# Attention followed by a gated MLP: one PSUM buffer of eight banks, two of them read side by side

## The chip, the core and the metric

The kernel runs on one core of one Trainium2 chip. The metric is device time in microseconds (us) of the one launch, as a median of several runs; smaller is better. The core has five engines with a queue each: PE multiplies matrices and writes its results to PSUM; ACT (ScalarE) and DVE (VectorE) read PSUM and write SBUF, the working memory; POOL (GpSimd) works on SBUF; SP issues DMAs. In this kernel PSUM is used as eight banks of 128 partitions by 512 fp32 columns. PE, ACT, DVE and POOL work their queues in program order, and wait for one another through semaphores.

## The reference

Grouped-query attention and then a gated MLP with a mixing over the sequence. Eight batches, 16 query heads in 4 groups, 384 positions, head size 64; the inner widths are 1024 and 512.

```python
scores = scale * np.matmul(q, k.transpose(0, 1, 3, 2))      # k, v repeated for the 4 heads of a group
attn = np.exp(scores - np.max(scores, axis=-1, keepdims=True))
attn = attn / (np.sum(attn, axis=-1, keepdims=True) + 1e-09)
x = np.matmul(attn, v)                    # heads side by side: (8, 384, 1024)
...
h = np.maximum(x @ w_in, 0.0)
u, v = h[..., :512], h[..., 512:]
v_n = (v - mu) / np.sqrt(var + 1e-06)     # mean and variance over the 512
v_s = np.einsum('ts,bsd->btd', w_spatial, v_n) + b_spatial[None, :, None]
return (u * v_s) @ w_out
```

## The kernel before

**Tiles.** A batch's attention is cut into six *sets*: three blocks of 128 query rows, times two pairs of key/value heads. One set has three *units*, one for each block of 128 keys. In a unit PE makes scores for the two halves of the pair (`hh` 0 and 1): two matmuls of 64 rows by 512 columns, one on rows 0 to 63 of the array and one on rows 64 to 127, so that they run side by side, each into a bank of its own (`sc`, L281). ACT takes the exponential of each bank into the tile `aT` (L293; no maximum is subtracted, which a count at the end of the kernel guards). `weigh` then multiplies `aT` with the values: 12 matmuls of 65 columns for each half into one bank `av` (L301); the 65th column of each head is the sum of the weights. DVE takes the reciprocals of these sums (L315) and multiplies (L317) into `x16`, which goes on to the MLP transposed, by PE for the first batch (`x_turn`), by a DMA on SP's queue for the others (`x_send`).

**The MLP is filler.** A generator (`gated`, L514) yields the MLP's matmuls one by one: `pv` (L357, the half that is normalized; DVE takes its relu and statistics), `pu` (L438; ACT takes the relu), `psp` (L457, the mixing over positions; DVE adds the bias, POOL multiplies by u) and `po` (L496, the output; DVE or ACT copies it, and SP sends it out). Each of these holds a bank from its first matmul until its reader is done, and `pour` (L727) stops in mid-accumulation wherever the share of work that it was given is used up.

**The order is written out by hand** (L53: the schedule is manual). The loop over the first 21 units (L749) issues a unit or two, then transposes and other things that are due, then weighs half a set, then pours. The loop after that (L774) goes by sets: the six score matmuls of a set; the three exponentials of half 0; a pour of 0.2 of a step's share; the weighing of the *second* half of the set before; a pour of 0.3; whatever is due; the three exponentials of half 1; a pour of 0.1; the weighing of the *first* half of this set; a pour of 0.4.

**Banks are planned.** `bank` (L79) gives out PSUM by a small clock of its own: it keeps for each bank when its reader will be done (`done`), takes the one that is done first, and moves PE's clock there if it isn't yet. `spend` (L87) moves PE's clock by a matmul's cost, `reads` (L90) the reader's. These costs only decide which bank is taken and how much is poured; on the chip the waits are semaphores. Each bank is a tile of its own with a tag, so a matmul that writes a bank waits for whatever read it last.

Of the kernel before, what the change touches and what calls it, by code (L numbers as in the profile page):

```python
# [18 lines left out]
def kernel(  # L19
# [14 lines left out]
    nc = tc.nc  # L34
    P = 128
    B, HQ, S, D = q.shape
# [18 lines left out]
    cst = ctx.enter_context(tc.tile_pool(name="cst", bufs=1))  # L55
# [5 lines left out]
    ps = order.enter_context(tc.tile_pool(name="ps", bufs=1, space=PSUM))  # L61
# [7 lines left out]
            name=nc.get_next_instruction_name(), act_func_set_id=set_id, ins=[], outs=[]  # L69
        )  # L70
    )
    pool, dve, act, sp = nc.gpsimd, nc.vector, nc.scalar, nc.sync


    clock = {nc.tensor: 7700.0, act: 0.0, dve: 0.0}
    done = [0.0] * 8
    taken = {}

    def bank(shape, dtype, name):  # L79
        i = min(range(8), key=done.__getitem__)  # L80
        t = ps.tile(shape, dtype, name=name, tag=f"bank{i}")
        clock[nc.tensor] = max(clock[nc.tensor], done[i])
        done[i] = 1e12 + clock[nc.tensor]
        taken[name] = i
        return t

    def spend(ns):  # L87
        clock[nc.tensor] += ns

    def reads(eng, ns, name=None):  # L90
        clock[eng] = max(clock[eng], clock[nc.tensor] + 200.0) + ns
        if name:
            done[taken.pop(name)] = clock[eng]

    C512, C384, C128 = 216, 162, 56

# [78 lines left out]
    v1 = [cst.tile([P, HKV, NT, VW], FP16, name=f"v1_{i}") for i in range(2)]  # L175
# [4 lines left out]
    k16s, q16s, kTs, qTs = {}, {}, {}, {}  # L180
# [35 lines left out]
    def copy(eng, o, i, name):  # L216
        reads(eng, 600.0 if name.startswith("po") else 430.0, name)
        (act.copy if eng is act else dve.tensor_copy)(o, i)  # L218
# [45 lines left out]
    aTs, x16s, xts = {}, {}, {}  # L264
    r_all = cst.tile([P, B * SETS * 2 * G], FP32, name="r_all")

    def units(u, count):
        b, r = divmod(u, UNITS)
        s, kt0 = divmod(r, NT)
        qt, j = divmod(s, 2)  # L270
        kts = range(kt0, kt0 + count)
        if kt0 == 0:
            aTs[b, s] = att.tile([P, NT, 2, G * P], FP16, name=f"aT_{b}_{s}", tag="aT", bufs=3)
        scs = [
            (kt, hh, bank([P, G * P], FP32, f"sc_{b}_{s}_{hh}_{kt}"))
            for hh in range(2)
            for kt in kts
        ]
        for kt, hh, sc in sorted(scs, key=lambda x: x[:2]):
            rows = slice(hh * D, (hh + 1) * D)  # L280
            nc.tensor.matmul(  # L281
                sc,
                kTs[b][rows, j, kt * P : (kt + 1) * P],
                qTs[b, j][rows, qt].rearrange("p (r i c) -> p i r c", r=G, i=G),
                start=True,
                stop=True,
            )
        spend(count * C512 + 186)
        return [(aTs[b, s][:, kt, hh], sc, f"sc_{b}_{s}_{hh}_{kt}") for kt, hh, sc in scs]

    def exp(a, sc, name):
        reads(act, 480.0, name)
        act.activation(a, sc, AF.Exp, scale=scale)  # L293

    def weigh(b, s, hh):
        qt, j = divmod(s, 2)
        aT = aTs[b, s]
        av = bank([P, 512], FP32, f"av_{b}_{s}_{hh}")
        for kt in range(NT):
            for i in range(G):  # L300
                nc.tensor.matmul(  # L301
                    av[:, i * (D + 1) : (i + 1) * (D + 1)],
                    aT[:, kt, hh, i * P : (i + 1) * P],
                    v1[b % 2][:, 2 * j + hh, kt, 0 : D + 1],
                    start=(kt == 0 and i == 0),
                    stop=(kt == NT - 1 and i == G - 1),
                )
        if s == 0 and hh == 0:
            x16s[b] = att.tile([P, NT, DM], FP16, name=f"x16_{b}", tag="x16")
        o = av[:, 0 : G * (D + 1)].rearrange("p (i d) -> p i d", i=G)  # L310
        spend(372)
        n = (b * SETS + s) * 2 + hh
        r = r_all[:, n * G : (n + 1) * G].rearrange("p (i a) -> p i a", a=1)
        reads(dve, 600.0, f"av_{b}_{s}_{hh}")
        dve.reciprocal(r, o[:, :, D : D + 1])  # L315
        c = j * 512 + hh * 256
        dve.tensor_tensor(  # L317
            x16s[b][:, qt, c : c + 256].rearrange("p (i d) -> p i d", i=G),
            o[:, :, 0:D],
            r.to_broadcast([P, G, D]),  # L320
            ALU.mult,
        )
        measure()

    def new_xt(b):
# [278 lines left out]
    def idle(count):  # L604
        name = f"idle_{idle_no[0]}"
        ps = bank([P, P], FP32, name)
        done[taken.pop(name)] = clock[nc.tensor] + 400.0
# [113 lines left out]
    ends = {}  # L721
# [25 lines left out]
    halves = {}  # L747
    TWO = 13
    for u in range(ALONE):  # L749
        if u < TWO or (u - TWO) % 2 == 0:  # L750
            pairs = units(u, 1)
            if u >= TWO and u + 1 < ALONE:
                pairs += units(u + 1, 1)
            for pair in pairs:
                exp(*pair)
        spare = 736 if u < TWO else (600 if (u - TWO) % 2 == 0 else 870)
        for f, args in todo.pop(u, []):
            f(*args)
            spare -= 224 if f in (q_turn, x_turn, k_turn) else 0
        for b, s in ends.pop(u, []):  # L760
            halves.setdefault(u, []).append((b, s, 0))
            halves.setdefault(u + (0 if s == 0 else 1), []).append((b, s, 1))
        for h in halves.pop(u, []):
            weigh(*h)
            spare -= 372
            if h[2]:
                turn_x(*h[:2], u)
        owed = pour(u, min(owed, 0) + spare)
    for u in sorted(halves):
        for h in halves[u]:  # L770
            weigh(*h)
    owed = 0.0
    late = [(b, s, hh) for u in (ALONE, ALONE + 1) for b, s in ends.pop(u, []) for hh in range(2)]
    for n in range(ALONE, total, NT):  # L774
        share = STEP * (0.85 if n < 90 else 1.0)
        exps = units(n, NT)
        for pair in exps[:NT]:
            exp(*pair)
        owed = pour(n, owed + share * F[0])
        for h in late:  # L780
            weigh(*h)
            if h[2]:
                turn_x(*h[:2], n)
        owed = pour(n, owed + share * F[1])
        for u in range(n, n + NT):
            for f, args in todo.pop(u, []):
                f(*args)
        for pair in exps[NT:]:
            exp(*pair)
# [7 lines left out]
    for h in late:  # L797
        weigh(*h)
        turn_x(*h[:2], n)
# [240 lines left out]
```

## Time and profile before

| | |
|---|---|
| time, median of 3 runs | 238.28 us (238.16 to 238.79) |
| time of the profiled execution | 238.65 us |
| its span, first to last instruction | 237.1 us |
| granted TensorE clock | 1.00 |
| instructions | 5954 |
| DMA traffic | 47.48 MB, mean 200 GB/s |

The span is 1.5 us shorter than the execution's time. The busy time in tenths, in 40 slices of 5.9 us each, shows how the engines are loaded over time:

| | |
|---|---|
| PE | 7899999999999999999999999999999999999993 |
| DVE | 2668774676447674566646576376744667367561 |
| ACT | 2899989959897869977797776986697776401212 |

In the first slices, up to some 30 us, ACT is as full as PE: many units, little filler. From there to some 200 us a step for each set repeats with a period of 4.0 to 4.6 us. After the last set only the MLP of the last two batches is left, and ACT is nearly idle. A row of a group in the profile gives an instruction's line, engine, what it writes and reads, its count, its total busy time and the mean of one in ns, then the idle time of the engine ahead of it and what ended that.

### The profile page before, as it was taken

Reading aid. Unit: us, or ns where it says so; the run is one execution under the profiler, and the core shown is the slowest. Engines: PE = TensorE matmul, PEld = TensorE weight load, DVE = VectorE, ACT = ScalarE, POOL = GpSimd, SP = SyncE. Lnnn points to the kernel's source line nnn. Section 1 sums busy time; section 2 is a strip of 40 time slices with the busy share of each in tenths; the row PEclk is TensorE's granted clock in tenths of the full one; section 3 lists DMA queues with packets and bytes.
Section 4 is the critical chain, followed back from the end, with each engine's and each line's share of the span. In section 5 each row is a group of like instructions: output and inputs, shape, how many; then the busy total and the mean of one; then the engine's idle time right before and its main releaser. Section 6 shows DMA issues by size and latency. Waiting matters only on the chain.

```text
span 237.1 us, 5954 instructions
## 1 busy us (share of the span) xinstructions
PE 230.4 (97%) x2317; PEld 124.3 (52%) x2317; DVE 143.8 (61%) x382; ACT 170.0 (72%) x350; POOL 102.2 (43%) x149
## 2 busy tenths in 40 slices
PE   7899999999999999999999999999999999999993
PEld 6555655545554545555464555554465455545542
DVE  2668774676447674566646576376744667367561
ACT  2899989959897869977797776986697776401212
POOL 3489493642556442275045800575032500460740
PEclk9999999999999999999999999999999999999999
DMA  6999959999999999699988899479912543240266
GB/s 186 289 300 308 275 152 160 169 317 260 296 211 237 258 351 171 214 199 309 188 257 214 241 214 294 68 271 158 255 27 44 114 164 79 48 177 0 86 229 222
DMA packets 67757, 47.48 MB, mean 200 GB/s; under 512 B 48368, under 2 KB 60576, under 8 KB 67728
## 3 DMA queue, kind: packets, MB, share of 16 engines
q1 hardware_dynamic: 62800, 39.86, 68.9%
q0 software_dynamic: 3952, 6.42, 12.3%
q10 hardware_dynamic: 976, 0.82, 1.1%
q8 instruction: 18, 0.29, 0.5%
q14 instruction: 11, 0.09, 0.1%
HBM read 25.95 MB, written 12.58 MB: 163 GB/s over the span
## 4 chain that ended last, share of the span: by engine, by line
PE 91%; DMA 4%; DVE 2%; issue 0%; ACTq 0%; ACT 0%
PE pu L438 18%; PE pv L357 17%; PE po L496 17%; PE sc L281 15%; PE av L301 14%; PE psp L457 7%; DMA q<-in_q_dram 2%; DMA qT<-q 2%; PE qps L240 1%; PE xps L334 1%; DVE x L317 1%; DVE qT L218 0%; DVE osb L218 0%; DVE q L208 0%; ACTq L124 0%
## 5 line engine op out<-in xcount | busy, mean ns | idle before, releaser
L293 ACT ACTIVATE aT<-sc 128x512 f16<-128x512 f32 x288 | 147.5, 617 | 31.4 <-PE sc L281 30.8
L301 PEld LDWEIGHTS <-aT 128*128 128x128 f16 x1152 | 47.0, 97 | 17.3 <-issue 2.3
L357 PE MATMUL pv<-w_in,xt 128*128 128x512 f16 x192 | 51.0, 380 | 0.1
L301 PE MATMUL av<-v,aT 128*128 128x65 f16 x1152 | 50.5, 193 | 0.1
L496 PE MATMUL po<-w_out,gT 128*128 128x512 f16 (+2 forms) x200 | 50.5, 371 | 0.0
L438 PE MATMUL pu<-xt,w_in 128*128 128x384 f16 x256 | 49.9, 327 | 0.0
L401 POOL TENSOR_SCALAR vn<-vr,rstd,nmr 128x512 f16<-128x512 f32 x23 | 17.6, 779 | 67.0 <-DVE nmr L396 45.6
L474 POOL TENSOR_TENSOR gT<-vs,uT 128x384 f16<-128x384 f32 x31 | 32.4, 1058 | 31.8 <-DVE r_all L315 16.9
L317 DVE TENSOR_TENSOR x<-av,r_all 128x256 f16<-128x256 f32 x96 | 40.7, 424 | 3.3
L281 PE MATMUL sc<-qT,kT 64*128 64x512 f16 x288 | 41.5, 380 | 0.3
L315 DVE RECIPROCAL r_all<-av 128x4 f32<-128x4 f32 x96 | 17.1, 178 | 40.6 <-PE av L301 40.3
L218 DVE COPY osb<-po 128x512 f32<-128x512 f32 (+2 forms) x39 | 26.1, 669 | 16.3 <-PE po L496 16.3
L438 PEld LDWEIGHTS <-w_in 128*128 128x128 f16 x256 | 22.1, 98 | 17.1 <-issue 5.5
L449 ACT ACTIVATE uT<-pu 128x384 f16<-128x384 f32 x32 | 15.8, 495 | 16.0 <-PE pu L438 15.8
L496 PEld LDWEIGHTS <-gT 128*128 128x128 f16 x200 | 17.6, 98 | 17.1 <-issue 3.3
L357 PEld LDWEIGHTS <-xt 128*128 128x128 f16 x192 | 15.8, 97 | 17.8 <-issue 5.5
L281 PEld LDWEIGHTS <-kT 64*128 64x128 f16 x288 | 10.9, 94 | 23.5 <-issue 11.9
L457 PE MATMUL psp<-wsT,vn 128*128 128x384 f16 x96 | 22.2, 327 | 0.0
L469 DVE TENSOR_TENSOR vs<-psp,bias_bc 128x384 f32<-128x384 f32 x32 | 17.6, 552 | 7.1 <-PE psp L457 6.9
L371 DVE TENSOR_SCALAR vr<-pv 128x512 f32<-128x512 f32 x24 | 16.4, 682 | 8.4 <-PE pv L357 8.3
L203 POOL CAST q<-q 128x768 f16<-128x768 f32 x22 | 17.6, 830 | 7.9 <-issue 4.3
L383 DVE BATCH_NORM_STATS2 stats<-vr 128x6 f32<-128x512 f32 x24 | 16.4, 685 | 0.1
(55 smaller groups left out, 103.2 us busy)
## 6 DMA issues: line engine op xcount, KB each, us to landing
out_dram<-osb SPq DMA_DIRECT2D x20, 512.0 KB, 3.9
q<-in_q_dram SPq DMA_DIRECT2D x10, 768.0 KB, 5.7
v_None<-in_v_dram SPq DMA_DIRECT2D x6, 384.0 KB, 7.0
w_in<-in_moe_w_in_dram POOLq DMA_DIRECT2D x4, 512.0 KB, 9.8
k_None<-in_k_dram SPq DMA_DIRECT2D x5, 384.0 KB, 3.8
out_dram<-osb SPq DMA_DIRECT2D x7, 256.0 KB, 2.5
q<-in_q_dram POOLq DMA_DIRECT2D x2, 768.0 KB, 7.6
w_out<-in_moe_w_out_dram POOLq DMA_DIRECT2D x2, 512.0 KB, 9.5
```

The costliest lines, as they stand in the source:

```text
L203: eng.tensor_copy(t16[:, :, :, hh, :], src[:, hh])
L218: (act.copy if eng is act else dve.tensor_copy)(o, i)
L281: nc.tensor.matmul(sc, kTs[b][rows, j, kt * P : (kt + 1) * P], qTs[b, j][rows, qt].rearrange("p (r i c) -> p i r c", r=G, i=G), start=True ...
L293: act.activation(a, sc, AF.Exp, scale=scale)
L301: nc.tensor.matmul(av[:, i * (D + 1) : (i + 1) * (D + 1)], aT[:, kt, hh, i * P : (i + 1) * P], v1[b % 2][:, 2 * j + hh, kt, 0 : D + 1], st ...
L317: dve.tensor_tensor(x16s[b][:, qt, c : c + 256].rearrange("p (i d) -> p i d", i=G), o[:, :, 0:D], r.to_broadcast([P, G, D]), ALU.mult,)
L357: nc.tensor.matmul(pv, xts[b][:, kt, st * P : (st + 1) * P], w_in16[:, kt, DH:DFF], start=(kt == 0), stop=(kt == NK - 1),)
L401: (dve if b == 0 and st == 1 else pool).tensor_scalar(vn, v_r.pop((b, st)), rstd[:, st : st + 1], nmr[:, st : st + 1], op0=ALU.mult, op1=A ...
L438: nc.tensor.matmul(pu[:, 0:S], w_in16[:, kt, m * P : (m + 1) * P], xts[b][:, kt, :], start=(kt == 0), stop=(kt == NK - 1),)
L457: nc.tensor.matmul(psp[:, 0:S], v_n[b, st][:, m * P : (m + 1) * P], wsT16[:, st, :], start=(st == 0), stop=(st == NT - 1),)
L474: pool.tensor_tensor(gT, vs, uT, ALU.mult)
L496: nc.tensor.matmul(po[:, 0:width], gTs[b][:, m, tt * P : (tt + 1) * P], w_out16[:, m, c0 : c0 + width], start=(m == 0), stop=(m == NM - 1),)
```

## The change

PSUM becomes one tensor of eight banks. `bank` gives out one of them, and now prefers, among those that its clock holds to be free, one whose neighbour will be busy longest. `pair` gives out two neighbours, or, if these would be free over 300 ns later than the two best, any two. A unit's two halves go into a pair, and one exponential reads both (1024 columns); where no neighbours were had, two exponentials do. `weigh` takes both halves of a set in a row into a pair, and DVE makes one reciprocal and one product of both. In the loop over sets the first two units' exponentials stand at the front and the third in the middle, and the whole set before is weighed in the one place where its second half was; the shares of filler 0.1 and 0.4 behind the last exponential become one of 0.5. In the first 21 units both halves are weighed at the unit where the first was. The planner's costs are 840 ns for a wide exponential (960 for two) and 900 ns for the wide reciprocal and product (1200 for two).

```diff
+    psum = ps.tile([P, 8, 512], FP32, name="psum")
...
     def bank(shape, dtype, name):
-        i = min(range(8), key=done.__getitem__)
-        t = ps.tile(shape, dtype, name=name, tag=f"bank{i}")
...
+        free = [i for i in range(8) if done[i] <= clock[nc.tensor]]
+        i = max(free, key=lambda i: done[i ^ 1]) if free else min(range(8), key=done.__getitem__)
+        hold(name, i)
+        t = psum[:, i]
...
+    def pair(name):
+
+        i = min(range(7), key=lambda i: max(done[i : i + 2]))
+        j, k = sorted(range(8), key=done.__getitem__)[:2]
+        if max(done[i : i + 2]) > max(done[k], clock[nc.tensor]) + 300.0:
+            hold(name, j, k)
+            return [psum[:, j], psum[:, k]], None
+        hold(name, i, i + 1)
+        return [psum[:, i], psum[:, i + 1]], psum[:, i : i + 2]
...
-    def exp(a, sc, name):
-        reads(act, 480.0, name)
-        act.activation(a, sc, AF.Exp, scale=scale)
-
-    def weigh(b, s, hh):
+    def exp(a, two, both, name):
+        if both is not None:
+            reads(act, 840.0, name)
+            act.activation(a, both, AF.Exp, scale=scale)
+        else:
+            reads(act, 960.0, name)
+            for hh in range(2):
+                act.activation(a[:, hh], two[hh], AF.Exp, scale=scale)
...
+    def weigh(b, s):
...
+        two, both = pair(name)
+        for hh in range(2):
+            for kt in range(NT):
+                for i in range(G):
+                    nc.tensor.matmul(
+                        two[hh][:, i * (D + 1) : (i + 1) * (D + 1)],
+                        aT[:, kt, hh, i * P : (i + 1) * P],
+                        v1[b % 2][:, 2 * j + hh, kt, 0 : D + 1],
...
+            dve.reciprocal(r[:, h0:h1], o[:, :, :, D : D + 1])
+            dve.tensor_tensor(
+                x[:, h0:h1], o[:, :, :, 0:D], r[:, h0:h1].to_broadcast([P, h1 - h0, G, D]), ALU.mult
+            )
...
         exps = units(n, NT)
-        for pair in exps[:NT]:
-            exp(*pair)
+        for x in exps[:2]:
+            exp(*x)
         owed = pour(n, owed + share * F[0])
-        for h in late:
-            weigh(*h)
-            if h[2]:
-                turn_x(*h[:2], n)
+        for x in late:
+            weigh(*x)
+            turn_x(*x, n)
         owed = pour(n, owed + share * F[1])
...
-        for pair in exps[NT:]:
-            exp(*pair)
-        owed = pour(n, owed + share * F[2])
-        late = []
-        for u in range(n, n + NT):
-            for b, s in ends.pop(u + 2, []):
-                weigh(b, s, 0)
-                late.append((b, s, 1))
-        owed = pour(n, owed + share * F[3])
+        for x in exps[2:]:
+            exp(*x)
+        owed = pour(n, owed + share * (F[2] + F[3]))
+        late = [x for u in range(n, n + NT) for x in ends.pop(u + 2, [])]
```

More of the change, by code (lines that the diff above doesn't have):

```diff
@@ L92, in reads @@
         if name:
-            done[taken.pop(name)] = clock[eng]
+            for i in taken.pop(name):
+                done[i] = clock[eng]
     C512, C384, C128 = 216, 162, 56
@@ L273, in units @@
             aTs[b, s] = att.tile([P, NT, 2, G * P], FP16, name=f"aT_{b}_{s}", tag="aT", bufs=3)
[L274 to L287, printed above, removed]
@@ L288, in units @@
-        spend(count * C512 + 186)
-        return [(aTs[b, s][:, kt, hh], sc, f"sc_{b}_{s}_{hh}_{kt}") for kt, hh, sc in scs]
-    def exp(a, sc, name):
-        reads(act, 480.0, name)
-        act.activation(a, sc, AF.Exp, scale=scale)
-    def weigh(b, s, hh):
+        scs = [(kt, *pair(f"sc_{b}_{s}_{kt}")) for kt in kts]
+        for kt, two, _ in scs:
+            for hh, sc in enumerate(two):
+                rows = slice(hh * D, (hh + 1) * D)
+                nc.tensor.matmul(
+                    sc,
+                    kTs[b][rows, j, kt * P : (kt + 1) * P],
+                    qTs[b, j][rows, qt].rearrange("p (r i c) -> p i r c", r=G, i=G),
+                    start=True,
+                    stop=True,
+                )
@@ new lines, in units @@
+        spend(count * C512 + 186)
+        return [(aTs[b, s][:, kt], two, both, f"sc_{b}_{s}_{kt}") for kt, two, both in scs]
+    def exp(a, two, both, name):
+        if both is not None:
+            reads(act, 840.0, name)
+            act.activation(a, both, AF.Exp, scale=scale)
+        else:
+            reads(act, 960.0, name)
+            for hh in range(2):
+                act.activation(a[:, hh], two[hh], AF.Exp, scale=scale)
+    r_all = cst.tile([P, B * SETS * 2 * G], FP32, name="r_all")
@@ L296, in weigh @@
+    def weigh(b, s):
         qt, j = divmod(s, 2)
         aT = aTs[b, s]
[L298 to L307, printed above, removed]
@@ L308, in weigh @@
-        if s == 0 and hh == 0:
-            x16s[b] = att.tile([P, NT, DM], FP16, name=f"x16_{b}", tag="x16")
[L310 to L322, printed above, removed]
+        name = f"av_{b}_{s}"
@@ new lines, in weigh @@
+        if s == 0:
+            x16s[b] = att.tile([P, NT, DM], FP16, name=f"x16_{b}", tag="x16")
+        spend(744)
+        n = (b * SETS + s) * 2 * G
+        r = r_all[:, n : n + 2 * G].rearrange("p (h i a) -> p h i a", h=2, a=1)
+        x = x16s[b][:, qt, j * 512 : j * 512 + 512].rearrange("p (h i d) -> p h i d", h=2, i=G)
+        reads(dve, 900.0 if both is not None else 1200.0, name)
+        for h0, h1, av in ((0, 2, both),) if both is not None else ((0, 1, two[0]), (1, 2, two[1])):
+            if both is None:
+                av = av.rearrange("p (h f) -> p h f", h=1)
+            o = av[:, :, 0 : G * (D + 1)].rearrange("p h (i d) -> p h i d", i=G)
+            dve.reciprocal(r[:, h0:h1], o[:, :, :, D : D + 1])
+            dve.tensor_tensor(
+                x[:, h0:h1], o[:, :, :, 0:D], r[:, h0:h1].to_broadcast([P, h1 - h0, G, D]), ALU.mult
+            )
@@ L606, in idle @@
         ps = bank([P, P], FP32, name)
-        done[taken.pop(name)] = clock[nc.tensor] + 400.0
+        for i in taken.pop(name):
+            done[i] = clock[nc.tensor] + 400.0
         idle_no[0] += 1
@@ L750 @@
         if u < TWO or (u - TWO) % 2 == 0:
-            pairs = units(u, 1)
+            exps = units(u, 1)
             if u >= TWO and u + 1 < ALONE:
-                pairs += units(u + 1, 1)
-            for pair in pairs:
-                exp(*pair)
+                exps += units(u + 1, 1)
+            for x in exps:
+                exp(*x)
         spare = 736 if u < TWO else (600 if (u - TWO) % 2 == 0 else 870)
@@ L760 @@
         for b, s in ends.pop(u, []):
[L761 to L767 removed]
+            weigh(b, s)
+            spare -= 744
+            turn_x(b, s, u)
         owed = pour(u, min(owed, 0) + spare)
[L769 to L771 removed]
     owed = 0.0
[L773 removed]
+    late = [x for u in (ALONE, ALONE + 1) for x in ends.pop(u, [])]
     for n in range(ALONE, total, NT):
```

28 lines of the change are left out of this document (18 added, 10 removed).

## The prediction

> **What bounds the kernel now.** First the page: busy time per engine, then the chain that ended last.
>
> ```profile
> PE 230.4 (97%) x2317; PEld 124.3 (52%) x2317; DVE 143.8 (61%) x382; ACT 170.0 (72%) x350; POOL 102.2 (43%) x149
> ...
> PE 91%; DMA 4%; DVE 2%; issue 0%; ACTq 0%; ACT 0%
> ```
>
> The engines that the change relieves, ACT (72%) and DVE (61%), are not on the chain; PE is 91% of it. A busy PE need not be a full one, so I looked at stretches:
>
> ```profile
> core 0: us, PE busy (x) PEld busy (x) DVE busy (x) ACT busy (x) POOL busy (x), PEclk, DMA share, GB/s
> 12.00:36.00 24.00, 23.85 (x318) 13.61 (x318) 18.66 (x56) 22.35 (x45) 19.23 (x34) 1.00 0.98 256
> 36.00:100.00 64.00, 63.72 (x687) 34.04 (x682) 37.55 (x106) 54.41 (x115) 27.50 (x36) 1.00 1.10 243
> 100.00:200.00 100.00, 100.00 (x1011) 51.86 (x1010) 62.09 (x162) 76.71 (x157) 36.48 (x46) 1.00 0.79 184
> ```
>
> PE has 100.00 us of work in 100.00, at a granted clock of 1.00. In the timeline's single records matmul starts are 216 ns apart for 512 columns, 162 for 384, 29 for 65; a block of three score pairs takes 0.75 us from its first start to the next matmul. Summed from 12 us to the end, the gaps beyond these spacings come to 2.9 us. So PE sets the pace, all its waits together are worth 2.9 us, and a new PE wait goes to the end undiminished.
>
> **Part 1: wide reads, fewer instructions.** The instruction order of the changed program has the same 2317 matmuls, 136 wide exponentials plus 8 pairs left as two, and 48 reciprocals and 48 normalizations in place of 96 each. Rows, by shape:
>
> ```profile
> L293 ACT ACTIVATE aT<-sc 128x512 f16<-128x512 f32 x288 | 147.5, 617 | 31.4 <-PE sc L281 30.8
> ...
> L317 DVE TENSOR_TENSOR x<-av,r_all 128x256 f16<-128x256 f32 x96 | 40.7, 424 | 3.3
> ...
> L218 DVE COPY osb<-po 128x512 f32<-128x512 f32 x37 | 25.4, 686 | 14.9 <-PE po L496 14.9
> ...
> L315 DVE RECIPROCAL r_all<-av 128x4 f32<-128x4 f32 x96 | 17.1, 178 | 40.6 <-PE av L301 40.3
> ...
> L218 ACT COPY osb<-po 128x512 f32<-128x512 f32 x10 | 5.9, 592 | 9.9 <-PE po L496 9.9
> ...
> L218 ACT COPY kT<-kps 128x384 f16<-128x384 f16 x1 | 0.5, 478 | 2.4 <-PE kps L226 2.4
> ...
> L218 DVE COPY osb<-po 128x256 f32<-128x256 f32 x1 | 0.4, 425 | 1.4 <-PE po L496 1.4
> ...
> L218 ACT COPY osb<-po 128x128 f32<-128x128 f32 x1 | 0.3, 266 | 0.1
> ```
>
> No row shows a 1024-wide exponential. ACT's copies give (592 − 266)/384 = 0.85 ns a column, so 605 (the median exponential) + 512 × 0.85 = 1.04 us. From below, the shortest exponential, 588, and the gentlest slope of ACT's copies ((478 − 266)/256 = 0.83) give 1.01; from above, one more back-to-back exponential: six take 3.04 us, (3.04 − 0.605)/5 = 0.487, so 1.09. I take 1.04, from the rows nearest in kind. Back to back that is 0.92 a pair against 0.974: 136 × 0.05 = 7 us off ACT. A normalization of 512 is 424 + (686 − 425) = 685 ns: 48 × (178 + 2 × 424 − 685) = 16 us off DVE. Neither is on the chain, so I book both at nothing; the cover is PE's 100 us in 100. Added are semaphore instructions ahead of some readers (47 on ACT that wait for DVE, on banks long free); ACT's 23 idle us of 100 hide them.
>
> Two things move on the readers' queues. ACT now has two wide exponentials ahead of the pours' relus, 2 × 0.92 against 3 × 0.487, so a relu, and with it the release of a pu bank, comes up to 0.4 us later; the third exponential follows after the poured work. And the half of a set that was weighed at the end of its own step is weighed one step later, with its normalization and the statistics that DVE issues behind it; the transposing DMA on SP's queue was already issued after the second half, so it stands where it stood. Both go to cover, unless a bank is late by them (part 3).
>
> **Part 2: banks, where the time goes.** In a set's step PE writes six score banks, pours two to four matmuls of the other layer, which hold a seventh bank open, and then weighs the set before.
>
> ```profile
> 134.72 0.82 PE L281 MATMUL sc<-qT,kT 64*128 64x512 f16 x6
> 135.47 0.60 PE L357 MATMUL pv<-w_in,xt 128*128 128x512 f16 x2
> 135.91 0.53 PE L301 MATMUL av<-v,aT 128*128 128x65 f16 x12
> ...
> 135.20 3.04 ACT L293 ACTIVATE aT<-sc 128x512 f16<-128x512 f32 x6 [1.57 <-PE sc L281]
> ```
>
> Now the weighing of half a set at 135.91 takes one bank, the eighth: no wait. Changed, it takes two at once: 6 + 1 + 2 = 9 of 8. The instruction order says which bank gives way: in 31 of the 41 full steps the first weighing matmul writes a bank that this same step's first score pair filled, and waits for that pair's exponential. When is it done? ACT starts 0.42 us after the first score matmul (76.06 to 76.48 in that step's timeline), or 0.48 where a semaphore instruction stands ahead (134.72 to 135.20); then 1.04; then 0.055 from a reader's end to the waiting matmul (single records near 54.6 and 55.1 us). That is 1.515 or 1.575 us after the block's start. PE gets there after 0.75 us plus the poured matmuls:
>
> - two of 512 columns, at 1.19: 6 steps, 5 with the semaphore: 0.32 + 5 × 0.38 = 2.2 us
> - three of 384, at 1.25: 14 steps, 6 with it: 8 × 0.27 + 6 × 0.33 = 4.1 us
> - 1.30 to 1.41 or 1.14: 11 steps, at 0.11 to 0.38: 2.0 us
>
> In sum 8.3 us. Queued behind the weighing matmul is all of PE; ACT, meanwhile, waits for nothing new and stands idle later, because the next scores come later. In seven other steps only the second half's bank is that of the fresh pair, 0.35 us on: covered to within 0.04.
>
> The Trainium skill has a rule here, Perfetto Trace Analysis, "Optimizing Scalar/DVE Operations": "If Scalar/Vector aren't saturated, but are causing bubbles on other engines, breaking up instructions may allow work to be completed sooner." It speaks against this change. Split, the first half's bank would be free at 0.42 + 0.605 + 0.055 = 1.08, before PE's 1.19, and the 8.3 us would fall to almost none; by the rows as the change has them it stays 8.3. No run here shows the split with these banks.
>
> **Part 3: the other waits that the bank choice makes**, by the same reckoning (matmuls between writer and waiter against latency plus reader):
>
> - three steps whose pair includes a bank just handed to DVE (vr once, vs twice): 0.73 + 0.60 + 0.60 = 1.9 us
> - two steps where the weighing ends just ahead of the score block, which then waits for the wide normalization: reciprocal and product last 0.22 + 0.685 = 0.905 us, with 0.23 ahead and 0.055 behind 1.19, against 0.56 of cover: 1.3 us
> - the first 21 units: four waits of a unit for the wide exponential just before it (0.36, 0.23, 0.37, 0.10), about 1.0 us
> - a bank taken again soon after its copy (po, psp, and four at the end at 0.09): 1.0 us
>
> This makes 5.2 us. Reckoned the same way, before has 1.0 us of such waits, which I take off; another 0.5 I take off for waits that fall right behind one another. The last set's transposing DMA has some 10 us of other PE work before the pv that needs it, so I book it at nothing; without that cover it would cost its whole flight.
>
> **Sum:** 8.3 + 5.2 − 1.0 − 0.5 = 12.0 us. The profiled execution took 238.65 us with a span of 237.1; 0.37 over the median 238.28. The forecast is 238.3 + 12.0, rounded to **250**.
>
> **Rivals.**
>
> 1. *Not slower.* Grouping pays because the early stretch goes at ACT's pace: 22.35 of 24.00 us busy from 12 to 36. There 18 pairs at 0.05 us give 0.9 us, and of PE's 2.9 us of waits perhaps half go: 238.3 − 0.9 − 1.4 = 236. The Trainium skill, Perfetto Trace Analysis, "Optimizing Scalar/DVE Operations", has this side too: grouping helps "if the engine is saturated", which by the row ACT nears only there. This rival holds if the pour's bank is closed when the pair is taken, or if a wide read ends before 1.19 − 0.42 − 0.055 = 0.72 us. Against it: the order names the waits one by one, and 0.72 is less than 1.01. Chance 0.10, of which same 0.04.
> 2. *Half the price.* The waits are there but shorter (readers nearer 1.01 us, waits merging): 31 × 0.10 + 2 = 5, so 243. For it: cover and latency differ by only 0.1 to 0.4 us. Chance 0.11.
> 3. *Chains of waits.* DVE's queue (copies of 686, statistics of 685 ns) stands ahead of the wide normalization, and a score block waits for it in more steps than the two: 0.3 us in 31 steps more, 9 us, so 259. Against: DVE is idle 38 of 100 us. Chance 0.06.
> 4. *It doesn't do what it says:* the planner could fall back on split pairs. The order has 8 of 144, so this is nearly out; it would bring rival 1 or 2 and is held in them.
>
> The forecast has 0.73. Its own range, from 1.01 to 1.09 us a wide read (31 × 0.03 down, 31 × 0.05 up) and part 3 halved or half again, is 245.5 to 255. To leave out no more than 2 in 10 (rivals 1 and 3, and the ends of the others) I go to 242.5 and 256. Faster or slower means by over 0.3% (0.7 us), what this kernel's spread of 238.16 to 238.79 can tell: faster 0.06, same 0.04, slower 0.90.
>
> **What would show it.** PE gaps of 0.1 to 0.4 us between the poured matmuls and the first av matmul, released by ACT's exponential of the same step; PE busy below 96 us of 100 in mid-kernel; wide exponentials near 1.04 us, normalizations near 0.69; ACT and DVE less busy by 7 and 16 us in all. Wrong, if PE is still gapless in mid-kernel, if av's wait ends on something else, or if the score blocks, not av, do the waiting.

## The result, and the profile after

The changed kernel takes 255.35 us (median of 6 runs, 255.13 to 256.57); the kernel before took 238.22 beside it (6 runs, 237.87 to 239.58). The ratio is 1.071, with a 95% interval of 1.0685 to 1.0735: 17.1 us slower, where 12.0 were forecast. The span of the profiled execution grew from 237.1 to 254.3 us at a granted clock of 1.00.

First the busy times, and the chain that ended last, of the changed kernel:

```profile
PE 237.6 (93%) x2317; PEld 124.5 (49%) x2317; DVE 133.1 (52%) x286; ACT 163.1 (64%) x214; POOL 101.4 (40%) x149
...
PE 73%; ACT 12%; DVE 8%; issue 2%; DMA 2%; POOL 1%; ACTq 0%; DVEq 0%; POOLq 0%
```

The two readers have less to do, ACT by 6.9 us and DVE by 10.7. Yet the chain, which was PE for 91%, now passes through ACT for 12% and through DVE for 8%: PE waits for readers that have less work than before. By stretches (columns as in the table of before):

```profile
core 0: us, PE busy (x) PEld busy (x) DVE busy (x) ACT busy (x) POOL busy (x), PEclk, DMA share, GB/s
12.00:36.00 24.00, 22.38 (x293) 12.74 (x294) 14.50 (x37) 20.92 (x25) 19.31 (x34) 1.00 1.04 256
36.00:100.00 64.00, 60.61 (x619) 30.81 (x618) 33.55 (x71) 45.84 (x61) 24.22 (x32) 1.00 0.97 221
100.00:200.00 100.00, 96.03 (x946) 48.70 (x943) 50.70 (x104) 70.70 (x91) 36.79 (x47) 1.00 0.75 183
```

The 100.00 busy us of mid-kernel have become 96.03, and 946 matmuls fit in where 1011 did. The groups that changed, with the row of the weighing before the change as the first line:

```profile
L301 PE MATMUL av<-v,aT 128*128 128x65 f16 x1152 | 50.5, 193 | 0.1
...
L316 ACT ACTIVATE aT<-psum 128x1024 f16<-128x1024 f32 x136 | 131.5, 1024 | 45.7 <-PE psum L303 45.6
L332 PE MATMUL psum<-v,aT 128*128 128x65 f16 x1152 | 43.0, 193 | 6.9 <-ACT aT L316 4.7
L350 DVE RECIPROCAL r_all<-psum 128x8 f32<-128x8 f32 x48 | 10.0, 208 | 60.9 <-PE psum L332 58.1
L351 DVE TENSOR_TENSOR x<-psum,r_all 128x512 f16<-128x512 f32 x48 | 33.2, 691 | 2.0 <-DVE r_all L350 0.3
```

A wide exponential lasts 1024 ns, the wide product 691, the wide reciprocal 208. The weighing's row (L301 before, L332 now) has what is new: PE stood idle 6.9 us ahead of its matmuls where it was 0.1, and 4.7 of this was for an exponential. ACT itself stood idle 45.7 us ahead of the exponentials, for scores that PE had not made yet. One ordinary step in the timeline:

```profile
154.41 0.82 PE L303 MATMUL psum<-qT,kT 64*128 64x512 f16 x6
155.16 0.66 PE L469 MATMUL psum<-xt,w_in 128*128 128x384 f16 x3
155.98 0.89 PE L332 MATMUL psum<-v,aT 128*128 128x65 f16 x24 [0.15 <-ACT aT L316]
...
154.90 1.94 ACT L316 ACTIVATE aT<-psum 128x1024 f16<-128x1024 f32 x2 [1.79 <-PE psum L303]
```

The scores begin at 154.41, three matmuls are poured from 155.16 on, and at 162 ns each the weighing is due at 155.65. It starts at 155.98, because its first bank is one that the exponential of 154.90 reads. (The bracket says 0.15, since the ends of matmuls are modelled. The stall is read from the starts: 0.31 us beyond the usual spacing from the last poured matmul.)

Counted so, as gaps beyond the usual spacing of starts, PE's stalls come to 8.9 us before and 26.3 after. That is 17.4 more, where the span grew by 17.2: the stalls went to the end undiminished. The count sums small excesses too, and gives 4.7 us after 12 us for the kernel before, where the prediction had 2.9; by gaps of 25 ns and more alone the two kernels still differ by 17.5 us there. From 12 us on, with what the waiting matmul waits for:

| PE's stalls after 12 us | us |
|---|---|
| 30 weighings, for an exponential of the same step | 9.6 |
| 2 weighings among the first units, likewise | 0.7 |
| 3 weighings, for a DVE reader of a bank just handed out | 2.1 |
| scores, for the normalization just ahead (2) or for another DVE reader | 2.1 |
| scores, for ACT; 1.65 of it in one step, at 43.6 us | 2.2 |
| MLP matmuls for DVE readers (copies, products, biases, relus) 1.9, turns 1.1, the mixing for POOL 0.5 | 3.4 |
| single ones below 25 ns, summed | 2.2 |
| sum (before: 4.7) | 22.3 |

### The profile page after: what moved, and what is told of

Its sections match the earlier page's. It is cut to its first block, busy times and chain, and to the rows that moved or that the text cites. A ratio compares the mean times of both kernels' runs of the same rounds, so it can differ in the third digit from the quotient of the medians.

```text
span 254.3 us, 5810 instructions
## 1 busy us (share of the span) xinstructions
PE 237.6 (93%) x2317; PEld 124.5 (49%) x2317; DVE 133.1 (52%) x286; ACT 163.1 (64%) x214; POOL 101.4 (40%) x149
## 4 chain that ended last, share of the span: by engine, by line
PE 73%; ACT 12%; DVE 8%; issue 2%; DMA 2%; POOL 1%; ACTq 0%; DVEq 0%; POOLq 0%
PE psum L527 16%; PE psum L388 16%; PE psum L332 15%; PE psum L303 10%; PE psum L469 10%; ACT aT L316 10%; PE psum L488 5%; DVE x L351 2%; DMA q<-in_q_dram 2%; DVE stats L414 2%; DVE r_all L350 1%; POOL vn L432 1%; ACT uT L480 1%; ACT rstd L420 1%; PE psum L265 1%
## 5 line engine op out<-in xcount | busy, mean ns | idle before, releaser
L316 ACT ACTIVATE aT<-psum 128x1024 f16<-128x1024 f32 x136 | 131.5, 1024 | 45.7 <-PE psum L303 45.6
L332 PEld LDWEIGHTS <-aT 128*128 128x128 f16 x1152 | 41.1, 97 | 20.7 <-issue 14.6
L527 PE MATMUL psum<-w_out,gT 128*128 128x512 f16 (+2 forms) x200 | 49.8, 371 | 0.2
L332 PE MATMUL psum<-v,aT 128*128 128x65 f16 x1152 | 43.0, 193 | 6.9 <-ACT aT L316 4.7
L388 PE MATMUL psum<-w_in,xt 128*128 128x512 f16 x192 | 48.6, 380 | 0.0
L469 PE MATMUL psum<-xt,w_in 128*128 128x384 f16 x256 | 47.8, 327 | 0.0
L303 PE MATMUL psum<-qT,kT 64*128 64x512 f16 x288 | 42.6, 381 | 2.6 <-DVE x L351 1.0
L243 DVE COPY osb<-psum 128x512 f32<-128x512 f32 (+2 forms) x39 | 25.8, 669 | 21.7 <-PE psum L527 19.6
L351 DVE TENSOR_TENSOR x<-psum,r_all 128x512 f16<-128x512 f32 x48 | 33.2, 691 | 2.0 <-DVE r_all L350 0.3
L500 DVE TENSOR_TENSOR vs<-psum,bias_bc 128x384 f32<-128x384 f32 x32 | 17.5, 553 | 8.7 <-PE psum L488 7.7
L488 PE MATMUL psum<-wsT,vn 128*128 128x384 f16 x96 | 21.6, 327 | 0.3 <-POOL vn L432 0.3
```

Of the source, the lines that this page charges most:

```text
L303: nc.tensor.matmul(sc, kTs[b][rows, j, kt * P : (kt + 1) * P], qTs[b, j][rows, qt].rearrange("p (r i c) -> p i r c", r=G, i=G), start=True ...
L316: act.activation(a, both, AF.Exp, scale=scale)
L332: nc.tensor.matmul(two[hh][:, i * (D + 1) : (i + 1) * (D + 1)], aT[:, kt, hh, i * P : (i + 1) * P], v1[b % 2][:, 2 * j + hh, kt, 0 : D + 1 ...
L351: dve.tensor_tensor(x[:, h0:h1], o[:, :, :, 0:D], r[:, h0:h1].to_broadcast([P, h1 - h0, G, D]), ALU.mult)
L388: nc.tensor.matmul(pv, xts[b][:, kt, st * P : (st + 1) * P], w_in16[:, kt, DH:DFF], start=(kt == 0), stop=(kt == NK - 1),)
L469: nc.tensor.matmul(pu[:, 0:S], w_in16[:, kt, m * P : (m + 1) * P], xts[b][:, kt, :], start=(kt == 0), stop=(kt == NK - 1),)
```

## Experiments: the three ways out of the ninth bank

The theory: a step needs nine banks of eight, and the weighing waits for a wide read to end. Three kernels each take away one of its parts: the width of the read, the short cover, and the second bank. The rival in each is that PE waits for ACT or DVE for some other reason.

**a_cut**: the first exponential of each full step is issued as two of 512 columns. Banks, planner and PE's order stay.

```diff
-            act.activation(a, both, AF.Exp, scale=scale)
+            if cut:
+                for hh in range(2):
+                    act.activation(a[:, hh], two[hh], AF.Exp, scale=scale)
+            else:
+                act.activation(a, both, AF.Exp, scale=scale)
...
-        for x in exps[:2]:
-            exp(*x)
+        for i, x in enumerate(exps[:2]):
+            exp(*x, cut=i == 0)
```

> The changed kernel, but in the loop over sets the first of the three wide exponentials of a step is issued as two of 512 columns. The planner's costs, the bank choice, PE's order and everything else stay. Theory 'nine banks' (the weighing's pair contains a bank that this step's first score pair filled, and waits for that pair's wide read): the first half's bank is free at 0.42 + 0.60 + 0.055 = 1.08 us after the block's start, before PE comes at 1.14 to 1.41, the second half's at about 1.56 against 1.49 to 1.75: of the 10.3 us that PE loses at the weighing for ACT, 7 to 8 go, 255.3 becomes 247 to 248.5. The cost of one more instruction on ACT a step is 0.05 us off PE's path. Rival 'ACT and DVE chains' (the weighing is late because ACT's and DVE's queues are late as a whole): two narrow instructions end no earlier as a pair than one wide, so 255 to 256. Rival 'one PSUM tensor' (reads of one tensor are serialized by semaphores however they are cut): 255 to 257.

Measured: 247.92 us, 1.041 (1.0374 to 1.0445) of the kernel before.

```profile
L320 ACT ACTIVATE aT<-psum 128x1024 f16<-128x1024 f32 x95 | 94.4, 1035 | 3.2 <-PE psum L303 3.0
L318 ACT ACTIVATE aT<-psum 128x512 f16<-128x512 f32 x82 | 44.5, 596 | 36.8 <-PE psum L303 36.7
L336 PE MATMUL psum<-v,aT 128*128 128x65 f16 x1152 | 43.5, 193 | 2.7 <-DVE vs L504 1.0 <-ACT aT L318 0.7 <-DVE vr L406 0.6
```

Forty-one wide reads have become 82 narrow ones of 596 ns, and the weighing's wait for them is down to 0.7 us in this view; its waits for wide ones, 0.4 us, are no longer among the three that the row names. By the starts, weighings that wait for an exponential go from 10.3 to 2.6 us, 7.7 less, and the time fell by 7.4. In the full steps 1.9 us are left of 9.6, 1.8 of them in four steps in which ACT was late as a whole (why, is shown below). More instructions on ACT, and a faster kernel: the rule of the Trainium skill that the prediction quotes, Perfetto Trace Analysis, "Optimizing Scalar/DVE Operations", on breaking up instructions of an engine that isn't saturated but holds up another, agrees with this run.

**a_late**: the wide reads stay, but the weighing comes after half of the step's filler.

```diff
-    F = (0.2, 0.3, 0.1, 0.4)
+    F = (0.5, 0.0, 0.1, 0.4)
```

> The changed kernel with the shares of filler ahead of and behind the weighing moved from 0.2 and 0.3 of a step to 0.5 and 0: the set before is weighed after 0.5 of a step's filler. Reads stay wide, pairs stay pairs. Theory 'nine banks': PE reaches the weighing 0.7 us later in the step, at 1.9 to 2.1 us, when the first wide read (1.5 us) has ended: 9 to 10 of the 10.3 us go, 255.3 becomes 245 to 247. Rival 'ACT and DVE chains': normalization and transposing DMA come 0.7 us later in each step, the score block waits for them more often: 255 or more. Rival 'one PSUM tensor': 255, since the number of semaphores is the same.

Measured: 245.41 us, 1.028 (1.0235 to 1.0325). Mid-kernel, in the view by stretches:

```profile
100.00:200.00 100.00, 99.52 (x995) 51.07 (x994) 56.63 (x117) 73.16 (x97) 37.27 (x47) 1.00 0.74 187
```

PE is nearly full again, with every wide read in place. Weighings that wait for ACT are 2.1 us in all, 8.2 less than in the changed kernel. The time fell by 9.9: the planner also comes to other banks here, and the wait at 43.6 us is gone. So in mid-kernel the wide read costs next to nothing by itself; it costs where PE comes back to the bank before it ends.

**a_halves**: a set is weighed in two places again, one bank and one normalization for each half, in the first 21 units too; the wide exponentials stay.

```diff
-        two, both = pair(name)
+        av = bank([P, 512], FP32, f"av_{b}_{s}_{hh}")
...
         for x in late:
-            weigh(*x)
-            turn_x(*x, n)
+            weigh(*x, 0)
         owed = pour(n, owed + share * F[1])
+        for x in late:
+            weigh(*x, 1)
+            turn_x(*x, n)
```

> The changed kernel with the weighing taken back to halves: one bank for each half, a normalization for each (96 of 256 columns), in the first 21 units at the units of before, in the loop over sets the first half where the changed kernel weighs and the second after the 0.3 of filler behind it. Exponentials stay wide and in pairs. Theory 'nine banks': the first half finds the eighth bank and waits for no exponential, the second comes 0.8 us later; the 10.3 us shrink to under 1, about 5 us of other waits on DVE stay or move: 244 to 247. Rival 'wide exponentials alone cost it' (a bank pair held 1.02 us by a wide read is what PE lacks, whatever the weighing takes): over 252.

Measured: 245.54 us, 1.0287 (1.025 to 1.0324). One weighing waits for ACT, 0.15 us. In their place ten wait for DVE, 3.8 us in sum: five of them take a bank that DVE has yet to read, for 0.67 to 0.78 us each. The new rule for single banks may have a part in this, but that is not shown: g_halves_apart below has the old rule, and 2.9 us of such waits. The ninth bank is gone, and part of it came back as another bank's wait. (The profiled execution, 247.0 us, was the longest of the four; 1.65 us of it is one MLP matmul at 59.5 us that waits for a transposing DMA.)

## Experiments: what else the change carries

After a_late 7 us were left. **b_one** is the kernel before with PSUM as one tensor, **b_policy** that with the new rule for single banks too; both keep the narrow reads.

```diff
+    psum = ps.tile([P, 8, 512], FP32, name="psum")
...
-        t = ps.tile(shape, dtype, name=name, tag=f"bank{i}")
+        t = psum[:, i]
```

```diff
-        i = min(range(8), key=done.__getitem__)
+        free = [i for i in range(8) if done[i] <= clock[nc.tensor]]
+        i = max(free, key=lambda i: done[i ^ 1]) if free else min(range(8), key=done.__getitem__)
```

> The kernel before with PSUM as one tensor of eight banks; bank choice, order, halves and narrow reads as before. Theory 'nine banks': one tensor adds semaphore instructions on ACT and DVE, on reads long done, which PE never sees: 238.2, ratio 0.998 to 1.002. Rival 'one PSUM tensor': part of the 17 us is here, 241 or more.

> As the run b_one, but single banks are chosen by the changed kernel's rule (of the free ones that whose neighbour is busy longest). Reckoned as in the prediction, banks taken again soon after their copy cost about 1.0 us more than before: 239 to 239.5, ratio 1.003 to 1.006. If the rule is harmless without pairs: 238.2.

Measured: b_one 238.94 us beside 238.57, ratio 1.000 (0.9974 to 1.0026): the one tensor costs nothing that can be seen. b_policy 240.22, 1.0068 (1.004 to 1.0096): the rule costs about 1.6 us beside the kernel before and 1.3 beside b_one, a little over what was expected. MLP matmuls that wait for a DVE reader go from 2 in the kernel before to 13 (0.19 to 1.55 us). Of all the banks that its clock calls free it takes the one whose neighbour is busy longest, which says nothing on how long the bank itself has been free; the old rule took the one that is done first.

The trace of after had shown one thing more, in two steps with a stall of 0.94 us. DVE, ACT and PE around one of them:

```profile
157.22 0.69 DVE L351 TENSOR_TENSOR x<-psum,r_all 128x512 f16<-128x512 f32 x1
157.82 0.68 DVE L414 BATCH_NORM_STATS2 stats<-vr 128x6 f32<-128x512 f32 x1
...
158.64 0.66 DVE L414 BATCH_NORM_STATS2 stats<-vr 128x6 f32<-128x512 f32 x1
159.34 0.18 DVE L415 BATCH_NORM_AGGREGATE mv<-stats 128x2 f32<-128x6 f32 x1
...
159.56 0.30 ACT L420 ACTIVATE rstd<-mv,eps_t 128x3 f32<-128x3 f32 x1 [0.54 <-DVE mv L415]
...
160.37 1.93 ACT L316 ACTIVATE aT<-psum 128x1024 f16<-128x1024 f32 x2
...
159.24 0.82 PE L303 MATMUL psum<-qT,kT 64*128 64x512 f16 x6
159.99 0.66 PE L469 MATMUL psum<-xt,w_in 128*128 128x384 f16 x3
161.43 0.25 PE L332 MATMUL psum<-v,aT 128*128 128x65 f16 x3 [0.78 <-ACT aT L316]
```

`measure`, which issues the statistics, is called behind a weighing. There is now one weighing a step, so two tiles' statistics stand back to back behind the normalization, at 157.82 and 158.64. ACT's `rstd`, two small activations that make a factor out of the statistics, needs them and starts at 159.56; behind it in ACT's queue stand a relu and the step's first exponential, which starts 1.13 us after its scores, not 0.43. **a_stats_same** issues the statistics right behind their relu; the planner's costs stay where they were, so PE's order and the banks are those of after. **a_stats** calls `measure` itself there, which moves the planner's costs too.

```diff
         unmeasured.append((b, st))
+        stats = small.tile([P, 6], FP32, name=f"stats_{b}_{st}", tag="stats")
+        dve.bn_stats(stats, v_r[b, st])
+        dve.bn_aggr(mvs[b][:, st], stats)
```

> The changed kernel with DVE's statistics of a v tile issued right behind its relu, not behind the next normalization of a weighed set. Theory 'late statistics': with one weighing a step two tiles' statistics stand in a row behind it, rstd on ACT waits for them (0.5 us idle each time) and the step's first exponential behind rstd starts at 1.13 instead of 0.43 us, which makes two weighing waits 0.94 instead of 0.25 us, and two or three more 0.2 to 0.4 longer, besides 0.5 us at a psp that waits for vn: 2 to 3 us go, 252.5 to 253.5. Rival (statistics between relu and reciprocal hold up the normalization as much as they gain): 255 to 256.

> The changed kernel with the statistics right behind the relu, as in the run a_stats, but with the planner's cost for them left where it was: PE's order, every bank and every wide read are those of the changed kernel, only two DVE instructions a tile move up. Theory 'late statistics': rstd no longer waits on ACT, the two weighing waits of 0.94 become 0.25, the 0.63, 0.47 and the 0.5 at psp shrink: 2 to 2.5 us go, 253. The rest of what a_stats gained (it came to 250.0) was then the planner's other banks. Rival 'all of it is the statistics': 250.

Measured: a_stats 250.04 us, 1.0485 (1.0454 to 1.0517), lower than expected; a_stats_same 252.74, 1.0577 (1.0528 to 1.0627), as expected. The same step in a_stats_same:

```profile
156.94 0.30 ACT L420 ACTIVATE rstd<-mv,eps_t 128x3 f32<-128x3 f32 x1
157.27 0.20 ACT L421 ACTIVATE rstd<-rstd 128x3 f32<-128x3 f32 x1
...
157.75 1.93 ACT L316 ACTIVATE aT<-psum 128x1024 f16<-128x1024 f32 x2
...
157.27 0.82 PE L303 MATMUL psum<-qT,kT 64*128 64x512 f16 x6
```

`rstd` no longer waits, and the exponential starts 0.48 us after the scores. The wait of 1.65 us at 43.6 us has the same cause. In after, `rstd` waits 1.92 us for the statistics, the two exponentials of a split pair stand behind it, and the next set's scores wait for their banks:

```profile
42.15 0.30 ACT L420 ACTIVATE rstd<-mv,eps_t 128x3 f32<-128x3 f32 x1 [1.92 <-DVE mv L415]
...
42.96 1.08 ACT L320 ACTIVATE aT<-psum 128x512 f16<-128x512 f32 x2
...
43.60 1.24 PE L303 MATMUL psum<-qT,kT 64*128 64x512 f16 x4 [0.85 <-ACT aT L320]
```

In a_stats_same this step has the same banks and the same split exponentials, and its six score matmuls run on from 41.96 us without a stall. So late statistics cost 2.6 us by the medians (3.1 by the spans). The other 2.7 us of a_stats (2.1 by the spans) aren't the statistics: there the planner came to other banks, and one weighing waits for a DVE reader, 0.35 us, where in a_stats_same four do, 2.8 us in sum.

## Experiments: can the wide reads pay?

**c_late_stats_old** puts the three remedies together: the weighing after half of the filler, early statistics, and the old rule for single banks.

```diff
-        free = [i for i in range(8) if done[i] <= clock[nc.tensor]]
-        i = max(free, key=lambda i: done[i ^ 1]) if free else min(range(8), key=done.__getitem__)
+        i = min(range(8), key=done.__getitem__)
...
-        if b == B - 1:
-            measure()
+        measure()
...
-    F = (0.2, 0.3, 0.1, 0.4)
+    F = (0.5, 0.0, 0.1, 0.4)
```

> Three edits on the changed kernel together: weighing after 0.5 of the filler, statistics right behind the relu, and single banks given out again to the one that is done first. Wide reads and pairs stay. If the waits named so far are independent and complete, of the 17.1 us the 9.9 of the late weighing, 2 of the statistics and 1 to 2 of bank reuse go: 241 to 243. If the wide reads have a cost of their own beyond these waits: 245 or more. Not below 238: PE's matmuls are the same and the first 21 units still weigh in pairs that wait for the unit before.

Measured: 241.96 us, 1.0128 (1.0082 to 1.0173), as expected. Of the 17.1 us, 13.7 are explained by what was taken back. Four more runs, all built on this one, looked for the rest. **d_solo_halves** weighs the first 21 units' sets by halves again; **e_solo_narrow** gives them narrow exponentials in single banks too, so that only the steps by sets are wide. **f_narrow_norm** is e with the halves in a row but in banks and normalizations of their own; **g_halves_apart** has them in two places again.

```diff
+            halves.setdefault(u, []).append((b, s, 0))
+            halves.setdefault(u + (0 if s == 0 else 1), []).append((b, s, 1))
+        for h in halves.pop(u, []):
+            weigh_half(*h)
...
-            exps = units(u, 1)
+            exps = units(u, 1, single=True)
...
-    F = (0.2, 0.3, 0.1, 0.4)
+    F = (0.4, 0.0, 0.20, 0.4)
```

(d: the first four lines, with F = (0.45, 0.0, 0.15, 0.4); e: all.) And f, then g, against e:

```diff
         for x in late:
-            weigh(*x)
+            weigh_half(*x, 0)
+            weigh_half(*x, 1)
             turn_x(*x, n)
```

```diff
-    F = (0.4, 0.0, 0.20, 0.4)
+    F = (0.3, 0.2, 0.1, 0.4)
...
         for x in late:
-            weigh(*x)
+            weigh_half(*x, 0)
+        owed = pour(n, owed + share * F[1])
+        for x in late:
+            weigh_half(*x, 1)
             turn_x(*x, n)
-        owed = pour(n, owed + share * F[1])
```

> The run c_late_stats_old with the weighing of the first 21 units taken back to halves at the units of before (one bank each), and the weighing of full steps after 0.45 of the filler. It tests what of the 3.4 us that c_late_stats_old still lacks sits in the first units: there it waits 0.85 us for the wide normalization ahead of x's first transposes and 0.33, 0.41, 0.32 for the exponential of the unit before. If these go, 239.5 to 240.5; if the first units run at ACT's pace and the waits only mirror it, 241.5 to 242.5.

> As d_solo_halves, and the scores of the first 21 units go into single banks with narrow exponentials, as before; weighing of full steps after 0.4 of the filler. So the first 30 us are those of before, and wide reads stand only where PE has filler. If the wide reads are worth something to PE anywhere, this should pass before: 237 to 238. If PE is the bound and gains nothing by them: 238.5 to 240.

> As e_solo_narrow, with only one thing more: the two halves of a set are still weighed in a row, but each into a single bank of its own with a reciprocal and a product of its own (178 and 424 ns) in place of the wide pair; the wide exponentials of the sets' steps stay. In e_solo_narrow three waits of a score block make 2.9 of the 4.0 us that PE waits from 12 to 110 us: 0.97 for a copy of qT (29.05), 0.72 and 1.20 for the wide normalization of the set weighed just ahead (31.81, 56.94). Theory (what is left over the kernel before is these few places where a score block follows soon on a wide weighing): the last two go or halve, time 238.8 to 240.2. Rival (what is left is spread over many steps, by wide exponentials): no change, 240.8 to 241.6.

> As f_narrow_norm, with the first half weighed after 0.3 of the filler and the second 0.2 later, so that each single bank has poured work on both sides. What is left of the change is then one PSUM tensor and the wide exponentials of the sets' steps. Theory: 238.3 to 239.8, at the kernel before within 0.5%; a time below 237.6 would say that a wide exponential is worth something to this kernel. Rival: 240.5 or more, and the wide exponentials alone cost it.

Measured, each beside the kernel before at 238.35 (d, e) and 238.73 (f, g):

| | us | ratio (95%) |
|---|---|---|
| d_solo_halves | 241.69 | 1.0136 (1.0095 to 1.0178) |
| e_solo_narrow | 241.17 | 1.0119 (1.0081 to 1.0157) |
| f_narrow_norm | 241.15 | 1.0088 (1.0059 to 1.0117) |
| g_halves_apart | 243.41 | 1.0175 (1.011 to 1.024) |

All four missed the times that my theory gave them, and d, f and g came out in the ranges of their rivals. The traces don't show the rivals' causes, though. In f, with wide exponentials in the steps by sets, PE is busy 100.00 us of the 100 from 100 to 200 us. In g the weighings wait 2.9 us for DVE and 0.2 for ACT. In d, ACT is busy 20.94 us of the 24 from 12 to 36, where it had 22.35 before, so it doesn't look as if these units went at ACT's pace. The stretches of e show where the rest isn't:

```profile
12.00:36.00 24.00, 22.50 (x300) 12.87 (x297) 17.26 (x50) 21.40 (x40) 18.35 (x33) 1.00 0.99 258
36.00:100.00 64.00, 62.42 (x665) 33.21 (x664) 33.29 (x71) 51.16 (x70) 27.03 (x35) 1.00 1.08 240
100.00:200.00 100.00, 100.00 (x1020) 51.82 (x1016) 58.84 (x121) 73.20 (x104) 36.88 (x46) 1.00 0.72 184
```

PE is full from 100 to 200 us. Most of what is missing against before, 1.35 and 1.30 busy us, lies ahead of 100. By the starts, e's stalls of 25 ns and more after 12 us come to 4.9 us against 2.0 before, and three score blocks, at 29.05, 31.81 and 56.94 us, hold 2.9 of them. The last of them, PE and then DVE:

```profile
54.22 0.90 PE L337 MATMUL psum<-v,aT 128*128 128x65 f16 x24
55.28 0.61 PE L305 MATMUL psum<-qT,kT 64*128 64x512 f16 x4 [0.17 <-ACT aT L318]
56.94 0.39 PE L305 MATMUL psum<-qT,kT 64*128 64x512 f16 x2 [1.04 <-DVE x L356]
...
54.42 0.69 DVE L437 TENSOR_SCALAR vr<-psum 128x512 f32<-128x512 f32 x1 [1.42 <-PE psum L423]
55.14 0.70 DVE L448 BATCH_NORM_STATS2 stats<-vr 128x6 f32<-128x512 f32 x1
...
56.20 0.69 DVE L356 TENSOR_TENSOR x<-psum,r_all 128x512 f16<-128x512 f32 x1
```

Here a weighing at 54.22 is followed by scores with nothing poured between, and its normalization stands behind a relu and, moved ahead now, that tile's statistics. f frees these banks by halves, and its time is the same: the waits at 31.81 and 56.94 for the wide product go, and 0.60 us at 56.48 for a wide exponential and 0.30 for a half's product come. g brings back 2.9 us of weighings that wait for DVE, as a_halves did. So a wide exponential in steps with enough filler is free here, but none of these versions gained from it. Most of what e lacks sits at two edges of the schedule, near 30 and 56 us; why f, which took two of the three waits away, got others in their place and no time back stays open.

## Why the prediction was right, point by point

**The time.** The way and the place of the loss are as forecast, but the loss is 17.1 us where the sum had 12.0. 255.35 us lies above the prediction's own range, 245.5 to 255, and within the wider one only by 0.65 us. (That own range is itself wider by some 1 us on each side than its terms make it: 31 × 0.03, 31 × 0.05 and half of 5.2 give 246.5 to 254.) That the limit of 256 held is luck: it was set so as to leave out no more than 2 chances in 10, not for a cost that then came. Without the late statistics the kernel takes 252.74 us (a_stats_same), inside both. Of the signs named, one was missed by a hair: PE is busy 96.03 us of 100 in mid-kernel, where below 96 was named.

**PE sets the pace, and its waits add up.** Right: 17.4 us of stalls more, 17.2 us of span.

**Part 1.** The prices held: 1024 ns against 1.04 us for the wide exponential, 691 against 685 for the product; ACT lost 6.9 of the forecast 7 us of work. DVE lost 10.7, not 16. The 16 was worked out wrongly: 178 + 2 × 424 − 685 counts one reciprocal of two and charges nothing for the wide one. With the measured rows, 2 × (178 + 424) − (208 + 691) = 305 ns, times 48, it is 14.6 us. DVE's groups, summed, agree (154.4 us before, 139.5 after); the busy time fell less because overlapping instructions count once there, and fewer of them overlap. No such figure was in the sum.

**"Both go to cover"** failed for the statistics. I named them as moved by a step and looked for a bank that is late by it; the one that waits is ACT's `rstd`, ahead of the exponentials in ACT's queue. It cost 2.6 us (a_stats_same), which the sum has at nothing. The other half, the relus' banks, did not show among the waits of the ordinary steps.

**Part 2, the nine banks of eight,** was right in its place, its mechanism and nearly its size. Thirty weighings wait, where 31 were named. In ordinary steps ACT started 0.43 or 0.49 us after the first score (0.42 or 0.48 forecast), and the weighing 1.51 or 1.57 us after it (1.515 or 1.575). The stalls are 0.31 to 0.37 behind two poured matmuls (0.32 to 0.38) and 0.25 to 0.34 behind three (0.27 to 0.33). In sum 9.6 us against 8.3; four steps in which ACT was late, with 0.47 to 0.95 each, are more than the difference, and with early statistics these four stand at 0.25 to 0.29 (a_stats_same). a_cut takes this wait alone away and gains 7.4 us.

**Part 3 is the term that was mis-sized.** Less the 1.5 us of deductions it stood at 3.7 us. Measured, all stalls other than the weighings' for ACT come to 12.0 us after 12 us, against 4.7 before: 7.3, and 8.0 with the two weighings among the first units. Some of its lines held: three banks just handed to DVE, 2.06 us against 1.9; two score blocks behind a wide normalization, 0.50 and 0.72 against 1.3. What I had not on the list: the score block at 43.6 us (1.65 us), which is late by the statistics again; a turn of `x` at 12.2 us that waits for the wide product (0.86); and many short waits of MLP matmuls for DVE readers (1.9), for which the new rule for single banks, 1.6 us in b_policy, is the likely cause.

**The rivals.** *Not slower* fell: with the ninth bank's waits gone PE gained nothing from fewer instructions, for PE was full before. *Half the price* fell with the sizes of single stalls. *Chains of waits* fell as stated, score blocks in 31 steps, but a smaller form of it is in the profile: ACT's queue behind DVE's statistics, and it is this that carried the time beyond the prediction's own range. *It doesn't do what it says* was nearly out, as the order had it; the one step with a split pair that stalled, at 43.6 us, runs without a stall in a_stats_same, split as before.

## What to carry to other kernels

Before an instruction is widened to read two banks, count the banks that are held at once in the tightest step: the price of a wide read is not its duration but that both banks come free at its end. If the count goes over, cut the first reader or put more filler ahead of the writer that comes back. Where an engine was not on the chain, taking work off it gained nothing here; and each operation that moves along with the edit has to be followed to whoever stands behind it in every queue, not only to the bank it reads.

## What was not expected of the hardware

A second reader in a row is cheap: one exponential of 512 columns takes 0.605 us, two in a row take 1.07 to 1.11 us together in the timelines of after and a_cut, and one of 1024 columns takes 1.02 to 1.03. Reading two banks at once saves ACT some 0.05 us. And eight banks as one tensor cost nothing beside eight tensors (1.000, 0.9974 to 1.0026), though DVE's queue then has 135 semaphore instructions in place of 63, and ACT's 62 in place of 48.
